# A second block of 1 to 32 slots in float32 on four column tiles, between the products of the first

## Chip, cores and metric

The kernel runs on one core of a Trainium2 chip. The metric is the device time of one execution in microseconds (us), the median of several runs. TensorE is PE in the profile (its weight loads are PEld), VectorE is DVE, ScalarE is ACT, GpSimd is POOL, and SyncE (SP) issues most of the DMAs.

## What is computed

Three stages follow one another: a linear attention over 2 x 768 tokens, a feed-forward layer with a leaky activation, and a mixture of 8 experts in which each token goes to one expert. The change touches the last stage only:

```python
logits = x @ w_gate                      # x: 1536 x 384, w_gate: 384 x 8
expert_idx = np.argmax(logits, axis=1)
...
for i in range(N):                       # capacity is 384 slots of an expert
    e = expert_idx[i]
    if counts[e] < capacity:
        disp[e, counts[e]] = x[i]
        ...
h = np.maximum(np.einsum('ecd,edf->ecf', disp, w1), 0.0)   # w1: 8 x 384 x 1024
y = np.einsum('ecf,efd->ecd', h, w2)                       # w2: 8 x 1024 x 384
out[i] = gate_w[i] * y[expert_idx[i], pos[i]]              # for the tokens kept
```

## The kernel before

Attention and the feed-forward layer run first, woven together. Each token's row, with its gate weight and its number, is scattered to `disp` in DRAM at the slot of its expert. One block of 128 slots of expert 0 is done early, beside the routing of the last tokens (class `Early`). Then a loop over the experts 0 to 7 (L1118) does the rest in blocks of 128 slots.

`expert(e, val)` runs the first block of an expert always, and a second and a third one only if the count on the chip, `val`, says so (`more`, the `tc.If` of L847, nested). Every engine reads the count into a register (`values_load`, L1125) and branches by itself. There is no loop on the chip: the code of all blocks stands in a row and is jumped over where it is not wanted.

`expert_block` works in two float32r parts (a high and a low part of each operand, three products for each pair, `PASS`). On PE a block is, in this order: `hidden(0)`, nine products of 128x128 by 512 columns (L775); five products of `hidden(1)`; `turn(0)`, four transposes (L784); the last four of `hidden(1)`; the transposes of the next expert's rows (`prep`, L658, `pd`); `second`, 24 products by 384 columns (L799) with `turn(1)` between them. ACT does the ReLU (L779) and the high part `hh` of the turned hidden values (L789), DVE their low part `hl` (L790) and at the end `y`, the output times the gate weight (L683), which POOL sends to `out` by an indirect DMA (L684).

Beside the first block of expert e the weights of expert e+1 are split into high and low parts: eight casts on ACT (L674) and eight differences on DVE and POOL (L677). The raw float32 weights (`re`) come by four DMAs of 768 KB for an expert (`load_expert`, L392 and L395), and behind them the expert's rows by one DMA (`load_rows`, L644, `drow`). All are issued in order by SP for expert e+2, ahead of expert e's own code; two experts' raw weights fit (even experts in one place, odd ones in another), so a load waits on SP until expert e's raw weights have been split. That happens during expert e-1.

The order on each engine is the order of the code (`manual_schedule`). A buffer that is used again makes its new writer wait for its last readers. In PSUM, the pool `acc` has four banks, `h` and `att` two each; in SBUF the tag `cv` has two buffers.

## Time and profile before

| what | value |
|---|---|
| median of 3 runs | 466.79 us (466.41 to 467.15) |
| the profiled execution | 466.23 us, span 464.5 us |
| PE busy | 437.4 us, 94% of the span |
| DVE, ACT, POOL busy | 271.0, 208.2, 157.7 us |
| the experts' loop (from expert 0's first product) | from 317.1 us on |

The page says how long each engine was busy and what its idle time waited for. PE is busy nearly throughout, so the time follows what PE has to do and the gaps in which it has nothing ready. Views that list instructions in order of time give a start, a length, and in brackets the idle time before them with what ended it; merged rows carry a count (x14). The length of a merged row runs to the end of its last instruction, and PE's products overlap, so the pitch of n products is the length less one product's own, over n - 1.

### The profile page before, as it was taken

Reading aid. Unit: us, or ns where it says so; the run is one execution under the profiler, and the core shown is the slowest. Engines: PE = TensorE matmul, PEld = TensorE weight load, DVE = VectorE, ACT = ScalarE, POOL = GpSimd, SP = SyncE. Lnnn points to the kernel's source line nnn. Section 1 sums busy time; section 2 is a strip of 40 time slices with the busy share of each in tenths; the row PEclk is TensorE's granted clock in tenths of the full one; section 3 lists DMA queues with packets and bytes.
Section 4 is the critical chain, followed back from the end, with each engine's and each line's share of the span. In section 5 each row is a group of like instructions: output and inputs, shape, how many; then the busy total and the mean of one; then the engine's idle time right before and its main releaser. Section 6 shows DMA issues by size and latency. Waiting matters only on the chain. (4 is left out here: it accounts for less than half of the span.)

```text
span 464.5 us, 7861 instructions
## 1 busy us (share of the span) xinstructions
PE 437.4 (94%) x3039; PEld 385.1 (83%) x3039; DVE 271.0 (58%) x470; ACT 208.2 (45%) x344; POOL 157.7 (34%) x138
## 2 busy tenths in 40 slices
PE   7977799699899999999999999999999999999995
PEld 6766699588788988989988888987988889898884
DVE  6998998999753444445333665354463535452651
ACT  1236634354344333323244444336473646553761
POOL 6855457464440231100300030033343515241660
PEclk9999979989999999999999999999999999999999
DMA  6999950649610207101700020018956556580200
GB/s 129 229 281 250 318 157 4 183 158 361 172 30 15 52 2 233 57 0 43 299 1 1 0 87 0 1 56 290 382 178 239 188 169 212 172 271 35 72 10 25
DMA packets 70605, 62.28 MB, mean 134 GB/s; under 512 B 41935, under 2 KB 58239, under 8 KB 70561
## 3 DMA queue, kind: packets, MB, share of 16 engines
q1 hardware_dynamic: 68832, 57.29, 41.1%
q0 software_dynamic: 1728, 4.40, 2.5%
q8 instruction: 28, 0.46, 0.4%
q14 instruction: 17, 0.13, 0.1%
HBM read 49.99 MB, written 12.62 MB: 135 GB/s over the span
## 5 line engine op out<-in xcount | busy, mean ns | idle before, releaser
L584 PE MATMUL acc<-wm,gh 128*128 128x384 f32 x384 | 102.0, 347 | 0.5 <-POOL wm L368 0.5
L599 PE MATMUL h<-xh,wm 128*128 128x512 f32 (+1 forms) x294 | 86.2, 402 | 4.4 <-DVE gl L622 4.4
L618 DVE SCALAR_TENSOR_TENSOR h<-ng,sign,h 128x512 f32<-128x512 f32 x48 | 36.1, 752 | 68.2 <-ACT ng L615 68.2
L584 PEld LDWEIGHTS acc<-wm,gh 128*128 128x128 f32 x384 | 69.9, 191 | 4.7 <-POOL wm L368 0.8
L775 PE MATMUL eh<-we,d 128*128 128x512 f32 x252 | 65.1, 403 | 4.5 <-PEq L847 3.2
L584 PE MATMUL acc<-wm,gl 128*128 128x384 f32 x192 | 65.4, 341 | 0.0
L599 PEld LDWEIGHTS h<-xh,wm 128*128 128x128 f32 x294 | 52.6, 190 | 14.2 <-issue 2.8
L615 ACT ACTIVATE ng<-h,slope 128x512 f32<-128x512 f32 x48 | 33.1, 689 | 60.1 <-PE h L599 60.0
L775 PEld LDWEIGHTS eh<-we,d 128*128 128x128 f32 x252 | 45.7, 188 | 15.5 <-issue 4.4
L619 ACT CAST gh<-h 128x512 fp32r<-128x512 f32 x48 | 28.1, 586 | 60.8 <-DVE h L618 60.8
L674 ACT CAST we<-re 128x768 fp32r<-128x768 f32 x64 | 50.6, 839 | 9.6 <-DMA re<-in_moe_w_dram 6.8
L677 POOL TENSOR_TENSOR we<-re,we 128x768 fp32r<-128x768 f32 x21 | 40.6, 1932 | 38.5 <-ACT we L674 32.2
L790 DVE TENSOR_TENSOR hl<-pht,hh 128x512 fp32r<-128x512 f32 x28 | 19.4, 692 | 51.6 <-ACT hh L789 49.8
L368 POOL TENSOR_TENSOR wm<-rm,wm 128x768 fp32r<-128x768 f32 x16 | 32.2, 2013 | 47.4 <-ACT wm L367 43.6
L799 PE MATMUL ey<-we,hh 128*128 128x384 f32 x224 | 48.1, 346 | 0.0
L677 DVE TENSOR_TENSOR we<-re,we 128x768 fp32r<-128x768 f32 x43 | 40.3, 965 | 11.9 <-ACT we L674 8.9
L522 POOL DMA_INDIRECT disp<-rows,sl x12 | 12.6, 1051 | 99.9 <-DVE run L543 64.4
L599 PE MATMUL h<-xl,wm 128*128 128x512 f32 (+1 forms) x147 | 42.1, 395 | 0.1
L622 DVE TENSOR_TENSOR gl<-h,gh 128x512 fp32r<-128x512 f32 x48 | 33.0, 687 | 15.6 <-ACT gh L619 15.6
L799 PEld LDWEIGHTS ey<-we,hh 128*128 128x128 f32 x224 | 37.8, 189 | 0.3 <-ACT hh L789 0.3
L584 PEld LDWEIGHTS acc<-wm,gl 128*128 128x128 f32 x192 | 36.6, 191 | 0.0
L599 PEld LDWEIGHTS h<-xl,wm 128*128 128x128 f32 x147 | 27.7, 191 | 7.0 <-DVE xl L270 0.3
(181 smaller groups left out, 618.8 us busy)
## 6 DMA issues: line engine op xcount, KB each, us to landing
re<-in_moe_w_dram SPq DMA_DIRECT2D x32, 768.0 KB, 7.2
rm<-in_moe_w_in_dram SPq DMA_DIRECT2D x8, 768.0 KB, 8.1
rm<-in_moe_w_out_dram SPq DMA_DIRECT2D x8, 768.0 KB, 7.5
disp<-rowss SPq DMA_DIRECT2D x1, 4825.0 KB, 16.0
drow<-disp SPq DMA_DIRECT2D x7, 579.0 KB, 3.9
out_dram<-rowss SPq DMA_DIRECT2D x1, 2304.0 KB, 22.4
kn<-in_k_dram SPq DMA_DIRECT2D x10, 192.0 KB, 4.6
rn<-in_r_dram SPq DMA_DIRECT2D x10, 192.0 KB, 4.8
```

Of the source, the lines that this page charges most:

```text
L368: eng.tensor_tensor(lo, low.bitcast(F32), hi.bitcast(F32), ALU.subtract)
L584: nc.tensor.matmul(accs[(blk, s)], gs[g][a][:, s * P:(s + 1) * P], wout[b][:, ft % 2, :], start=(ft == 0 and n == 0), stop=(ft == NFT - 1 ...
L599: nc.tensor.matmul(phs[g][:, cols[0]:cols[1]], win[a][:, c, o:o + P], xs[b][:, c, cols[0]:cols[1]], start=(n == 0), stop=(n == 3 * DC - 1))
L615: nc.scalar.activation(ng, ph, AF.Relu, scale=slope[:, ft:ft + 1])
L618: nc.vector.scalar_tensor_tensor(ph, ng, sign[:, ft:ft + 1], ph, op0=ALU.mult, op1=ALU.add)
L619: nc.scalar.copy(gh, ph)
L622: nc.vector.tensor_tensor(gl, ph, gh.bitcast(F32), ALU.subtract)
L674: nc.scalar.copy(t[:, sl], src[:, sl])
L677: le.tensor_tensor(t[:, sl2], src[:, sl], t[:, sl].bitcast(F32), ALU.subtract)
L775: nc.tensor.matmul(ph[q], d[x][:, c, :], ww[y][:, c, :], start=(n == 0), stop=(n == 3 * DC - 1))
L790: nc.vector.tensor_tensor(hl, pt, hh.bitcast(F32), ALU.subtract)
L799: nc.tensor.matmul(py, hT[q][x][:, c * P:(c + 1) * P], ww[y][:, c, :], start=(q == 0 and not low and c == 0 and y == 0), stop=(q == 1 and ...
```

## The change

A block of few slots gets a form of its own. Where the count of an expert is above 128 and at most 160, its second block (1 to 32 slots) is computed from the raw float32 weights, without high and low parts:

- `prep` copies the first 32 columns of the second block's turned rows to `dS` (DVE, one copy for each expert).
- `Short.hidden`: the 1024 hidden values of 32 slots are made as four column tiles of PE, each 32 columns of the array wide and each with 256 of the hidden values: 12 float32 products of 128x32 by 256 columns. `Short.relu` (ACT) and `Short.turn` (two transposes on PE, a DVE copy) prepare the second layer.
- `Short.second`: eight float32 products of 128x32 by 384 columns, again on four tiles, each tile a quarter of the sum over the hidden values. ACT copies the four quarters to `part`, and `Short.gather` adds them by one more product with `sel`, a matrix of four unit matrices that POOL makes at the start. Then a `y` of 32 rows and an indirect DMA.
- These steps stand between the steps of the first block's `front` (its `hidden` and `turn(0)`). `rest` is what is left of a block.
- `counts` now holds 0 for 129 to 160 slots and the count plus one otherwise (three small DVE operations more). Each expert branches on it in front of its first block: If (0) runs `front` with `Short`, Else runs `front` alone. So the code of the front stands there twice. The test for further blocks is `val > b * P + 1`; it fails for 0.
- `load_expert(e + 2)` and `load_rows(e + 2)` move from ahead of expert e to behind its front, since `Short` reads the raw weights that the load overwrites.

```diff
-                nc.vector.tensor_scalar(counts, pt[:, 0:E], float(cap), None, op0=ALU.min)
-                nc.vector.scalar_tensor_tensor(counts[:, 0:1], pt[:, 0:1], float(cap), sofar[:, 0:1],
+                c, few = cnt[:, 0], cnt[:, 1]
+                nc.vector.tensor_scalar(c, pt[:, 0:E], float(cap), None, op0=ALU.min)
+                nc.vector.scalar_tensor_tensor(c[:, 0:1], pt[:, 0:1], float(cap), sofar[:, 0:1],
                                                op0=ALU.min, op1=ALU.subtract)
+                nc.vector.scalar_tensor_tensor(few, c, float(P + CW), c, op0=ALU.is_le, op1=ALU.mult)
+                nc.vector.tensor_scalar(few, few, float(P), None, op0=ALU.is_le)
+                nc.vector.scalar_tensor_tensor(counts, c, 1.0, few, op0=ALU.add, op1=ALU.mult)
...
+            if b == 1:
+                dS[e] = p2.tile([P, DC, CW], F32, tag="ds", name=f"ds{e}")
+                nc.vector.tensor_copy(dS[e], src[:, :, 0:CW])
...
-    def put(rows, b, acc, name):
+    def put(rows, b, acc, name, n=P):
...
-        nc.vector.tensor_scalar(y, acc, rows[:, b, DM:DM + 1], None, op0=ALU.mult)
-        ins = nc.gpsimd.indirect_dma_start(out, bass.IndirectOffsetOnAxis(rows[:, b, DM + 1:DM + 2].bitcast(I32), 0), y, None,
-                                           bounds_check=NT - 1, oob_is_err=False)
+        nc.vector.tensor_scalar(y[0:n], acc[0:n], rows[0:n, b, DM:DM + 1], None, op0=ALU.mult)
+        ins = nc.gpsimd.indirect_dma_start(out, bass.IndirectOffsetOnAxis(rows[0:n, b, DM + 1:DM + 2].bitcast(I32), 0), y[0:n],
+                                           None, bounds_check=NT - 1, oob_is_err=False)
...
+        ph = [bank(f"eh{nm}_{q}", "h") for q in range(2)]
+        h = {0: p2.tile([P, HF], F32, tag="ng", name=f"hs{nm}_0")}
+        hT = {0: [p3.tile([P, HF], F32R, tag=t, name=f"{t}{nm}_0") for t in ("gh", "gl")]}
...
+        def front(few=None):
+            if few:
+                few.hidden()
+            hidden(0, 0, 3 * DC)
+            if few:
+                few.relu()
+            also(0)
+            relu(0)
+            if few:
+                few.turn()
+            hidden(1, 0, 5)
+            put_h0 = turn(0)
+            if few:
+                few.second()
+            also(1)
+            put_h0()
+            hidden(1, 5, 3 * DC)
+            if few:
+                few.gather()
+        def rest():
+            also(2)
+            relu(1)
+            also(3)
+            py = ps_acc.tile([P, DM], F32, tag="acc", name=f"ey{nm}")
+            second(py, 0, False, range(3))
+            put_h1 = turn(1)
+            put_h1()
+            second(py, 0, False, range(3, HF // P))
+            second(py, 0, True)
+            also(4)
+            second(py, 1, False)
+            second(py, 1, True)
+            put(dsp[e], b, py, nm)
+        return front, rest
+    class Short:
+        def __init__(self, e):
+            self.e = e
+            self.w = [raws[("e", e, q)].rearrange("p (c f) -> p c f", c=DC if q < 2 else HF // P) for q in range(NPIECE)]
...
+        def hidden(self):
+            n = F2 // NCT
+            self.ph = bank(f"eh{self.e}_s", "acc")
+            for c in range(DC):
+                for j in range(NCT):
+                    q, o = j * n // HF, j * n % HF
+                    nc.tensor.matmul(self.ph[j * CW:(j + 1) * CW, 0:n], dS[self.e][:, c, :], self.w[q][:, c, o:o + n],
+                                     start=(c == 0), stop=(c == DC - 1), skip_group_check=True)
+        def relu(self):
+            n = F2 // NCT
+            self.h = p2.tile([P, DM], F32, tag="cv", name=f"hs{self.e}_s")[:, 0:n]
+            nc.scalar.activation(self.h, self.ph[:, 0:n], AF.Relu)
+        def turn(self):
+            n = F2 // NCT
+            pt = bank(f"pht{self.e}_s")
+            for c in range(n // P):
+                nc.tensor.transpose(pt[:, c * P:(c + 1) * P], self.h[:, c * P:(c + 1) * P], ident)
+            self.hT = p2.tile([P, DM], F32, tag="cv", name=f"hT{self.e}_s")[:, 0:n]
+            nc.vector.tensor_copy(self.hT, pt[:, 0:n])
+        def second(self):
+            n = F2 // NCT // P
+            self.pp = bank(f"ey{self.e}_s", "acc")
+            for c in range(n):
+                for j in range(NCT):
+                    k = j * n + c
+                    nc.tensor.matmul(self.pp[j * CW:(j + 1) * CW, 0:DM], self.hT[:, c * P + j * CW:c * P + (j + 1) * CW],
+                                     self.w[2 + k * P // HF][:, k % (HF // P), :],
+                                     start=(c == 0), stop=(c == n - 1), skip_group_check=True)
+            self.part = p2.tile([P, DM], F32, tag="cv", name=f"part{self.e}")
+            nc.scalar.copy(self.part, self.pp[:, 0:DM])
+        def gather(self):
+            py = bank(f"es{self.e}")
+            nc.tensor.matmul(py[0:CW, 0:DM], sel, self.part, start=True, stop=True)
+            put(dsp[self.e], 1, py[:, 0:DM], f"{self.e}_s", CW)
...
-        expert_block(e, 0, beside)
+        front, rest = expert_block(e, 0, beside)
+        with tc.If(val < 1) as cmp:
+            front(Short(e))
+        with cmp.Else():
+            front()
+        if e + 2 < E:
+            for q in range(NPIECE):
+                load_expert(e + 2, q)
+            load_rows(e + 2)
+        rest()
 
         def more(b):
-            with tc.If(val > b * P):
+            with tc.If(val > b * P + 1):
                 got = []
-                expert_block(e, b, {2: [lambda: got.append(prep(e, b + 1))], 4: [lambda: got[0]()]} if b + 1 < SB else {})
+                for f in expert_block(e, b, {2: [lambda: got.append(prep(e, b + 1))], 4: [lambda: got[0]()]} if b + 1 < SB else {}):
+                    f()
...
+        nc.gpsimd.tensor_tensor(sel, ident[:, 0:CW], ident[:, CW:2 * CW], ALU.add)
+        for j in range(2, NCT):
+            nc.gpsimd.tensor_tensor(sel, sel, ident[:, j * CW:(j + 1) * CW], ALU.add)
...
         for e in range(E):
             if e + 1 < E:
                 claim(e + 1)
-            if e + 2 < E:
-                for q in range(NPIECE):
-                    load_expert(e + 2, q)
-                load_rows(e + 2)
-            val = nc.values_load(counts[0:1, e:e + 1], min_val=0, max_val=NT)
+            val = nc.values_load(counts[0:1, e:e + 1], min_val=0, max_val=1 + NT)
             expert(e, val)
```

On PE, expert 2's first block, before (eh: hidden products, pht: turned hidden values, pd: next expert's rows turned, ey: output):

```order
L1125 TENSOR_LOAD counts_105
L775 MATMUL eh2_0_0_3776<-we2_0_3470,d0_2_3468 128x512 x6
L775 MATMUL eh2_0_0_3776<-we2_0_3470,d1_2_3469 128x512 x3
L775 MATMUL eh2_0_1_3792<-we2_1_3471,d0_2_3468 128x512 x5
L784 MATMUL pht2_0_0_3798<-ident_87,hs2_0_0_3790 128x128 x4
L775 MATMUL eh2_0_1_3792<-we2_1_3471,d0_2_3468 128x512
L775 MATMUL eh2_0_1_3792<-we2_1_3471,d1_2_3469 128x512 x3
L658 MATMUL pd3_0_3813<-ident_87,drow3_3480 128x128 x3
L658 MATMUL pd3_1_3817<-ident_87,drow3_3480 128x128 x3
```

and after, the If side (eh2_s, pht2_s, ey2_s and es2 are the short block's):

```order
L1212 TENSOR_LOAD counts_105
L923 COMPARE_AND_BRANCH
L869 MATMUL eh2_s_3930<-re2_0_3326,ds2_3727 32x256 x12
L788 MATMUL eh2_0_0_3924<-we2_0_3553,d0_2_3551 128x512 x6
L788 MATMUL eh2_0_0_3924<-we2_0_3553,d1_2_3552 128x512 x3
L881 MATMUL pht2_s_3959<-ident_87,hs2_s_3952 128x128 x2
L788 MATMUL eh2_0_1_3925<-we2_1_3554,d0_2_3551 128x512 x5
L798 MATMUL pht2_0_0_3969<-ident_87,hs2_0_0_3926 128x128 x4
L892 MATMUL ey2_s_3974<-re2_2_3329,hT2_s_3962 32x384 x8
L788 MATMUL eh2_0_1_3925<-we2_1_3554,d0_2_3551 128x512
L788 MATMUL eh2_0_1_3925<-we2_1_3554,d1_2_3552 128x512 x3
L900 MATMUL es2_3993<-part2_3983,sel_107 32x384
```

The short block's products stand in four places of the first block's front, its first ones at the very start of the expert. The second block's own code is still there, behind the test of L934.

On SP, the loads for expert 7 before, issued ahead of expert 5's count and branches:

```order
L392 DMA re7_0_4594<-in_moe2_w1_dram 128x3x512 x2
L395 DMA re7_2_4597<-in_moe2_w2_dram 128x4x384 x2
L644 DMA drow7_4600<-disp_107 128x3x386
L1125 TENSOR_LOAD counts_105
L1125 ISA x2
```

and after:

```order
L1212 TENSOR_LOAD counts_105
L1212 ISA x2
L923 COMPARE_AND_BRANCH
L923 UNCONDITIONAL_BRANCH x2
L396 DMA re7_0_5091<-in_moe2_w1_dram 128x3x512 x2
L399 DMA re7_2_5094<-in_moe2_w2_dram 128x4x384 x2
L654 DMA drow7_5097<-disp_109 128x3x386
L934 COMPARE_AND_BRANCH x2
```

The four weight loads and the rows' load behind them have moved past the branch of expert 5's front; they now also wait for PE to have left that front.

On ACT, the start of expert 2 before (we3: the next expert's weights, hs: ReLU, hh: high part):

```order
L1125 TENSOR_LOAD counts_105
L674 CAST we3_0_3750<-re3_0_3474 128x768 x2
L779 ACTIVATE hs2_0_0_3790<-eh2_0_0_3776 128x512
L674 CAST we3_1_3751<-re3_0_3474 128x768
L789 CAST hh2_0_0_3803<-pht2_0_0_3798 128x512
```

and after, the If side:

```order
L1212 TENSOR_LOAD counts_105
L923 COMPARE_AND_BRANCH
L875 ACTIVATE hs2_s_3952<-eh2_s_3930 128x256
L687 CAST we3_0_3906<-re3_0_3679 128x768 x2
L793 ACTIVATE hs2_0_0_3926<-eh2_0_0_3924 128x512
L896 COPY part2_3983<-ey2_s_3974 128x384
L687 CAST we3_1_3907<-re3_0_3679 128x768
L804 CAST gh2_0_0_3927<-pht2_0_0_3969 128x512
```

The short block's ReLU now stands ahead of the first casts, and its copy of the quarters ahead of the cast and of the first block's high part.

## Rows read from the trace of the kernel before

**Rows 1.** The page: busy time of PE, and its granted clock in 40 slices
```profile
PE 437.4 (94%) x3039; PEld 385.1 (83%) x3039; DVE 271.0 (58%) x470; ACT 208.2 (45%) x344; POOL 157.7 (34%) x138
PEclk9999979989999999999999999999999999999999
```

**Rows 2.** Busy time by stretch (experts 1, 6); columns: length, then each engine, clock, DMA
```profile
337.70:358.20 20.50, 19.70 (x109) 17.50 (x109) 9.83 (x14) 11.78 (x20) 7.75 (x5) 1.00 0.66 219
438.80:449.60 10.80, 10.18 (x56) 8.91 (x56) 7.84 (x11) 9.08 (x14) 7.39 (x5) 1.00 0.04 13
```

**Rows 3.** PE in order of time (start, length, idle before): expert 1, expert 2's start
```profile
337.68 3.50 PE L775 MATMUL eh<-we,d 128*128 128x512 f32 x14 [0.79 <-PEq L847]
...
341.38 1.17 PE L775 MATMUL eh<-we,d 128*128 128x512 f32 x4
...
347.66 1.56 PE L775 MATMUL eh<-we,d 128*128 128x512 f32 x6
...
358.24 2.11 PE L775 MATMUL eh<-we,d 128*128 128x512 f32 x8 [0.84 <-PEq L847]
```

**Rows 4.** PE in order of time: expert 6, of one block, and expert 7's start
```profile
438.83 3.54 PE L775 MATMUL eh<-we,d 128*128 128x512 f32 x14 [0.59 <-ACTq L847]
...
443.59 0.82 PE L658 MATMUL pd<-ident,drow 128*128 128x128 f32 x6
...
449.61 2.61 PE L775 MATMUL eh<-we,d 128*128 128x512 f32 x10 [0.59 <-ACTq L847]
```

**Rows 5.** The page's groups: hidden products, ACT's casts (count, busy us, mean ns, idle)
```profile
L775 PE MATMUL eh<-we,d 128*128 128x512 f32 x252 | 65.1, 403 | 4.5 <-PEq L847 3.2
...
L674 ACT CAST we<-re 128x768 fp32r<-128x768 f32 x64 | 50.6, 839 | 9.6 <-DMA re<-in_moe_w_dram 6.8
```

**Rows 6.** PE in order of time: float32 products of the attention, whole array and parts
```profile
18.09 1.13 PE L218 MATMUL py<-S,rT 128*128 128x96 f32 x8 [0.49 <-ACT kT L202]
...
20.81 1.16 PE L209 MATMUL pa<-scratch,kT 64*128 64x128 f32 x16
...
25.95 0.64 PE L236 MATMUL pg<-scratch,kd 128*64 128x48 f32 x16
26.51 1.16 PE L209 MATMUL pa<-rT,scratch 64*128 64x128 f32 x16
...
30.38 1.14 PE L225 MATMUL py<-scratch,scratch 128*64 128x48 f32 x32
```

**Rows 7.** The source lines of two of them: shortest, median and longest in ns
```profile
L209 PE MATMUL pa<-scratch,kT x16: 272/272/373, 20.8 to 21.7; 64*128 64x128 f32 x16
L225 PE MATMUL py<-scratch,scratch x32: 222/222/257, 30.4 to 31.3; 128*64 128x48 f32 x32
```

**Rows 8.** The source view of L847: the compare and branch on PE's sequencer, in ns
```profile
L847 PEldq COMPARE_BRANCH  x18: 70/181/339, 325.6 to 457.5; - x18
```

**Rows 9.** DVE and POOL in order of time at expert 6's start: the end of expert 5
```profile
439.08 0.61 DVE L683 TENSOR_SCALAR y<-ey,drow 128x384 f32<-128x384 f32 x1
...
441.04 1.52 POOL L684 DMA_INDIRECT out_dram<-y,drow  x1 [0.16 <-issue]
```

**Rows 10.** DVE's groups by shape: a small copy
```profile
L448 DVE COPY lg<-pl 128x8 f32<-128x8 f32 x8 | 1.3, 159 | 2.2 <-PE pl L446 2.2
```

**Rows 11.** The source view of L684: landing times of the output DMAs
```profile
DMA to landing us min/median/max: 2.1/3.2/7.4
```

**Rows 12.** The source view of L392, 405 to 415 us: two loads for expert 7
```profile
DMA to landing us min/median/max: 4.6/5.3/6.1
```

**Rows 13.** The source view of L392, 315 to 316 us: two loads behind others
```profile
L392 SPq DMA_DIRECT2D re<-in_moe_w_dram x2: 487/488/488, 315.3 to 315.9; - x2
...
DMA to landing us min/median/max: 8.3/9.1/9.8
```

**Rows 14.** The page's DMA issues: KB of each, us to landing
```profile
re<-in_moe_w_dram SPq DMA_DIRECT2D x32, 768.0 KB, 7.2
...
drow<-disp SPq DMA_DIRECT2D x7, 579.0 KB, 3.9
```

More of the change, by code (lines that the diff above doesn't have):

```diff
@@ L100 @@
     counts = const.tile([P, E], I32, name="counts")
+    cnt = const.tile([P, 2, E], F32, name="cnt")
+    sel = const.tile([P, CW], F32, name="sel")
     sofar = const.tile([P, 2], F32, name="sofar")
@@ L784, in turn @@
                 nc.tensor.transpose(pt[:, c * P:(c + 1) * P], h[q][:, c * P:(c + 1) * P], ident)
-            hh = p3.tile([P, HF], F32R, tag="gh", name=f"hh{nm}_{q}")
-            hl = p3.tile([P, HF], F32R, tag="gl", name=f"hl{nm}_{q}")
+            if q not in hT:
+                hT[q] = [p3.tile([P, HF], F32R, tag=t, name=f"{t}{nm}_{q}") for t in ("gh", "gl")]
+            hh, hl = hT[q]
             def f():
```

33 lines of the change are left out of this document (6 added, 27 removed).

## The prediction, made before the run

> **What bounds the kernel now.** I read the page first: PE is busy 94% of the span and its granted clock is full in all late slices [rows 1], so time is what PE executes plus its gaps. Then the stretches of the experts: in expert 1, of two blocks, PE is busy 19.70 of 20.50 us and no other engine over 11.78; in expert 6, of one block, PE 10.18 of 10.80 and ACT 9.08 [rows 2]. The reader should see that PE is the bound in both, but that ACT has little room in an expert of one block. PE's list of instructions gives the steps: expert 1 runs from 337.68 to 358.24, 20.56 us, its second block begins at 347.66 without a gap, and the next expert begins 0.84 after PE fell idle, put down to the branch [rows 3]. Expert 6 runs from 438.83 to 449.61, 10.78 us with its gap of 0.59 [rows 4].
>
> Which experts change is in the data: the reference's own inputs route, after expert 0's early block and the cut at 384, 256, 132, 159, 141, 384, 57, 118 and 53 tokens to experts 0 to 7. So experts 1, 2 and 3 have second blocks of 4, 31 and 13 slots, all of them within 32; expert 4 keeps three blocks and expert 0 two.
>
> **What is removed.** A second block with its share of the gap is 20.56 - 10.78 = 9.78 us on PE. Three make 29.3.
>
> **What PE gets instead.** Price of one column first. In float32r, 14 products of 512 columns take 3.50 [rows 3], one alone 0.403 [rows 5]: a pitch of (3.50 - 0.40)/13 = 0.238, or 0.465 ns a column. A float32 product leaves two records. On two row tiles, 16 records of 128 columns take 1.16 us and one alone 0.272 [rows 6, 7]: eight pairs, (1.16 - 0.27)/7 = 0.127 for a pair, at most 0.99 ns a column if two run at once. On the whole array eight records of even fewer columns (96) take 1.13 [rows 6], a pitch of (1.13 - 0.27)/7 = 0.122 for one record against 0.064 for one on tiles. So tiles do run at once, nearly two for one. No row shows four tiles or a float32 product long enough to separate its columns from its weight load; a column is between 0.465 and 0.99 ns for each record. I take 0.93, twice the float32r price, as the nearest float32 row is close to it.
>
> With four at once: hidden, 3 rounds x 2 records x 256 x 0.93 = 1.43. Second layer, 2 x 2 x 384 x 0.93 = 1.43. Gather, 2 x 384 x 0.93 = 0.71. Two transposes at (0.82 - 0.27)/5 = 0.11 [rows 4], 0.22. Going from one division of the array to another: the last record of L236 starts near 25.95 + 0.64 - 0.22 = 26.37 and L209 begins at 26.51 [rows 6, 7], 0.14 instead of a pitch of 0.03, so 0.11 each; six of them, 0.66. Together 4.45 for an expert, 13.35 for three. At 0.465 a column it would be 2.66.
>
> The trace shows 1.9 of 2 for two tiles. The Trainium skill (TensorE: Matmul & The Clock Gate, Measured speedup vs the span model) gives 2.38 for three column tiles of 32, 0.79 of the ideal; by that the 2.86 of hidden and second layer would be 3.6 and the total 2.3 later, an estimate that no run here shows.
>
> **The new branch.** All eight experts now branch on PE ahead of their first product, right behind the count's load, when PE has run dry. One takes 0.18, at most 0.34 [rows 8]; the target lies behind some 30 to 90 instructions. I take 0.25, together 2.0. The ends are nothing (PE's sequencer is ahead of the array where 347.66 follows without a gap) [rows 3] and twice 0.34 for two branches, 5.4. The jump at the front's end has four products queued ahead of it and costs nothing; without that cover it is within the same bound.
>
> **Waits that the short block brings.** (1) Its hidden products stand first and take a bank of the pool `acc`, eight allocations to an expert on four banks, so it is the bank of the previous expert's output, free only after `y`. That ends at 439.08 + 0.61 = 439.69, 0.86 after expert 6's start [rows 9, 4]. Ahead of it DVE now has the copy of `dS`: 96 elements, between a copy of 8 (0.16) [rows 10] and `y` of 384 (0.61), by interpolation 0.27. PE is ready 0.25 after the old start, so it waits about 0.9, with all of the expert queued behind. This holds in experts 2 and 3, whose predecessor ends with that block: 1.8. Expert 1's predecessor had a second block since, so nothing. Ends: 0 and 3.
> (2) `hT` takes a `cv` buffer from which the previous `y` is still being sent: POOL starts that DMA 2.2 after the expert's start [rows 9, 4] and it lands 3.2 later, from 2.1 to 7.4 [rows 11]: at 5.4, from 4.3 to 9.6. DVE wants the buffer some 5.8 after the start (0.9, the short hidden, nine products, two transposes, two differences on DVE). I take nothing; the other end is 3.8 in each of two experts, with the first block's `hl` behind it on DVE.
> (3) ACT's copy of the quarters (at most 0.61) waits for the second layer, and a cast of 0.84 [rows 5] and `hh` stand behind it; PE has four products, the gather and six transposes for that time. I take nothing, at most 0.6 in each of three.
> DVE's three operations on the counts lie beside the early block's products, POOL's three for `sel` beside the attention's first loads; at the start of PE's work each would cost no more than a `y`.
>
> **The loads that moved.** Before, the loads for expert 7 were issued at 406.7 [rows 12], within expert 4. Now SP waits until PE has left expert 5's front, 341.38 + 1.17 - 337.68 = 4.87 after its start [rows 3]. The first piece lands after 4.6 [rows 12]. Loads in a queue land one behind the other: two issued 0.5 apart land after 8.3 and 9.8, so 2.0 apart [rows 13]. The fourth lands after 10.6, and the rows, 579 against 768 KB [rows 14], 1.5 later, 12.1. That is 17.0 after expert 5's start. Expert 6 wants the rows for its `pd` at 443.59 - 438.83 = 4.76 after its own start [rows 4], which is 10.78 + 0.25 later: 15.8. PE waits 1.2 there, with the first block's second layer behind it. The weights are earlier than ACT's casts want them. Ends: 0, and 5 if the first piece takes 8.3 [rows 13]. In experts 1 to 3 the loads start about 8 after an expert's start and have 15.5 of its length: the rows land near 20, wanted at 20.5 or later, so no wait. Expert 4 has three blocks of cover.
>
> **The sum.** -29.3 + 13.35 + 2.0 + 1.8 + 1.2 = -10.95. The profiled execution took 466.23 us with a span of 464.5; the median is 0.56 above it, and I take the difference from the median: 466.79 - 10.95 = 455.8.
>
> **Rivals.** Cheaper columns: at 0.465 ns three experts save 3 x 1.79 = 5.4 more, 450.4. For it: the float32 rows bound a column only from above. Against it: L209's pair stands close to 0.99.
> Two tiles at once, not four: hidden and second layer double, 3 x 2.86 = 8.6, 464.4. For it: no row has more than two.
> One tile after another, the case on the other side: 12 and 8 products instead of 3 and 2 rounds, 5.71 each, 3 x 8.56 = 25.7 more, 481.5. It decides from 10.95/3 = 3.65 us more for an expert, that is 6.5 for what would be 11.4 in a row: fewer than 1.75 tiles at once. Against it stand 0.064 and 0.122 [rows 6].
> Late data: the bounds of the output DMA or of the loads come true in part, 4 to 7 more, near 461.
> A jump that must fetch code: were each of the eight branches to wait for a DMA, at the shortest landing of 2.1 [rows 11], 8 x 2.1 = 16.8 instead of 2.0, 470.6. Against it: the jump over an unexecuted block in expert 6's end is inside a gap of 0.59 [rows 4]. The Trainium skill (Runtime: NRT & Kernel Launch, Instruction fetch mechanics) states that a taken branch to a page not loaded waits for a fetch.
> The short form is not taken, if the chip counts otherwise: 466.79 + 2.0 + 1.2 = 470.
>
> **How the numbers follow.** Forecast 0.60, cheaper columns 0.13, two at once 0.09, late data 0.08, one after another 0.05, fetch 0.03, not taken 0.02. A measurement here tells about 0.2% from no change. The first four are faster by more, 0.90, less 0.01 for the mishaps of two at once and late data together that end near 466: faster 0.89, same 0.02, slower 0.09. The range 449.5 to 464.0 holds the forecast (alone 453 to 459), cheaper columns, late data and the better half of two at once.
>
> **What would show it.** Right: 11 full blocks in the hidden products' count (198 instead of 252 for L775's successors), experts 1 to 3 lasting 15.5, 16.4 and 16.4, four records of a short product starting within hundredths of a microsecond, a wait of PE for `y` at the start of experts 2 and 3, and one for `drow` of about 1.2 in expert 6. Wrong: short products whose records follow one another, gaps over 1 us at the branch, or a wait for `re`.

## The result, and the profile after

The changed kernel takes 462.03 us (median of five runs, 461.06 to 463.93) where the kernel before took 467.08 on the same chip: a ratio of 0.9897, 95% interval 0.9872 to 0.9923. It is faster by 5.0 us; the sum of the prediction said 10.95. The profiled execution took 462.03 us, with a span of 459.9.

The page of the changed kernel first: busy time of the engines, PE's granted clock in 40 slices, and the group of the full blocks' hidden products (count, busy us, mean ns, idle before).

```profile
PE 424.0 (92%) x3012; PEld 363.5 (79%) x3012; DVE 267.9 (58%) x475; ACT 201.7 (44%) x335; POOL 160.0 (35%) x141
...
PEclk9998999989999999999999999999999899899999
...
L788 PE MATMUL eh<-we,d 128*128 128x512 f32 x198 | 54.5, 420 | 5.4 <-ACT we L687 3.1
```

Beside [rows 1, 5]: 198 hidden products stand where 252 stood, so three second blocks did take the short form. PE is busy 13.4 us less, but its share of the span went down from 94 to 92%, so waits came; the mean of one hidden product went from 403 to 420 ns, and two late slices of the clock are below 9, which before had none.

PE in order of time, experts 1 to 4 (start, length, idle before and what ended it), beside [rows 3]. L869 is the short block's hidden layer, L892 its second layer, L788 the full block:

```profile
337.67 1.50 PE L869 MATMUL eh_s<-re,ds 128*32 128x256 f32 x24 [0.99 <-DVEq L934]
...
343.22 1.50 PE L892 MATMUL ey_s<-re,hT_s 128*32 128x384 f32 x16
...
353.92 1.62 PE L869 MATMUL eh_s<-re,ds 128*32 128x256 f32 x24 [1.89 <-DVEq L934]
...
361.84 2.10 PE L892 MATMUL ey_s<-re,hT_s 128*32 128x384 f32 x16 [2.15 <-DVE hT_s L883]
...
373.84 1.50 PE L869 MATMUL eh_s<-re,ds 128*32 128x256 f32 x24 [1.66 <-DVEq L934]
...
380.24 1.50 PE L892 MATMUL ey_s<-re,hT_s 128*32 128x384 f32 x16 [0.78 <-DVE hT_s L883]
...
392.12 5.04 PE L788 MATMUL eh<-we,d 128*128 128x512 f32 x14 [3.08 <-ACT we L687]
```

Expert 1 lasts 16.25 us from start to start (15.5 forecast), expert 2 19.92 and expert 3 18.28 (16.4 forecast for each); expert 4 takes 30.37, 1.6 more than before. The short block itself is as forecast: 24 records in 1.50 us. What is new stands in the brackets. In experts 2 and 3 the second layer waits for the turned hidden values, and these, on DVE, for the DMA of `y`, which POOL had issued 6.2 us earlier in expert 2 (from 355.17 to 361.36) and 4.7 us earlier in expert 3; ACT's copy is held behind that. The last two rows are SP's, the loads of expert 4's weights:

```profile
355.17 1.00 POOL L697 DMA_INDIRECT out_dram<-y,drow  x1 [0.16 <-issue]
...
361.36 0.42 DVE L883 COPY hT_s<-pht_s 128x256 f32<-128x256 f32 x1 [2.61 <-DMA out_dram<-y,drow]
379.76 0.42 DVE L883 COPY hT_s<-pht_s 128x256 f32<-128x256 f32 x1 [1.10 <-DMA out_dram<-y,drow]
...
364.04 0.48 ACT L896 COPY part<-ey_s 128x384 f32<-128x384 f32 x1 [5.50 <-PE ey_s L892]
...
352.15 1.10 SPq L396 DMA_DIRECT2D re<-in_moe_w_dram  x2
353.30 1.23 SPq L399 DMA_DIRECT2D re<-in_moe_w_dram  x2
```

Stretches of PE (length, busy time of PE, PEld, DVE, ACT and POOL, then PE's granted clock, DMA share, GB/s): the wait in expert 2, what came behind it, expert 4's first products, and a stretch of expert 4 later on.

```profile
358.00:361.80 3.80, 1.68 (x10) 1.16 (x8) 1.17 (x2) 0.54 (x1) 0.00 (x0) 1.00 1.05 399
362.60:366.00 3.40, 3.40 (x17) 1.33 (x10) 0.23 (x1) 1.70 (x3) 0.66 (x1) 0.50 0.59 179
...
393.30:396.70 3.40, 3.40 (x9) 2.68 (x9) 0.41 (x1) 1.31 (x2) 0.41 (x1) 0.50 0.90 313
404.00:414.00 10.00, 10.00 (x57) 8.95 (x56) 3.83 (x7) 3.05 (x6) 2.84 (x2) 1.00 0.06 22
```

The clock is at its lower level, 1.2 GHz, in two stretches, each behind a wait of PE: the 2.15 us in expert 2 and the 3.08 at expert 4's start. There 14 products take 5.04 us instead of 3.50 [rows 3]. The first row also shows the DMA engines full (a share of 1.05) while the output DMA is on its way: expert 4's weights had been issued in the 3 us ahead of it.

The 3.08 us at expert 4 are put down to ACT, but ACT had only its usual casts. The source view of the branch (PE's queue, ns) and the instruction queue's DMA between 389.4 and 390.6 us (packets, MB, share) show what PE did then:

```profile
L923 PEldq COMPARE_BRANCH  x1: 2307/2307/2307, 389.6 to 389.6; - x1
```
```profile
q8 instruction: 1, 0.02, 5.6%
```

PE's own branch took 2.31 us, with one packet of code moving in the first half of it; its other ten L923 branches took 0.07 to 0.33.

### The profile page after: what moved, and what is told of

It is laid out like the page before. It is cut to its first block, busy times and chain, and to the rows that moved or that the text cites. A ratio compares the mean times of both kernels' runs of the same rounds, so it can differ in the third digit from the quotient of the medians.

```text
span 459.9 us, 7878 instructions
## 1 busy us (share of the span) xinstructions
PE 424.0 (92%) x3012; PEld 363.5 (79%) x3012; DVE 267.9 (58%) x475; ACT 201.7 (44%) x335; POOL 160.0 (35%) x141
## 5 line engine op out<-in xcount | busy, mean ns | idle before, releaser
L593 PE MATMUL acc<-wm,gh 128*128 128x384 f32 x384 | 100.8, 343 | 0.5 <-POOL wm L372 0.5
L608 PE MATMUL h<-xh,wm 128*128 128x512 f32 (+1 forms) x294 | 87.4, 407 | 3.6 <-DVE gl L631 3.6
L593 PEld LDWEIGHTS acc<-wm,gh 128*128 128x128 f32 x384 | 68.8, 188 | 4.9 <-POOL wm L372 1.1
L788 PE MATMUL eh<-we,d 128*128 128x512 f32 x198 | 54.5, 420 | 5.4 <-ACT we L687 3.1
L690 POOL TENSOR_TENSOR we<-re,we 128x768 fp32r<-128x768 f32 x21 | 41.7, 1984 | 50.8 <-ACT we L687 36.0
L788 PEld LDWEIGHTS eh<-we,d 128*128 128x128 f32 x198 | 37.2, 197 | 17.3 <-issue 9.9
L805 DVE TENSOR_TENSOR gl<-pht,gh 128x512 fp32r<-128x512 f32 x22 | 15.2, 692 | 44.1 <-ACT gh L804 42.4
L813 PE MATMUL ey<-we,gh 128*128 128x384 f32 x176 | 37.7, 346 | 0.0
L813 PEld LDWEIGHTS ey<-we,gh 128*128 128x128 f32 x176 | 29.7, 189 | 0.4 <-ACT gh L804 0.4
```

Source lines behind the costliest of these rows:

```text
L593: nc.tensor.matmul(accs[(blk, s)], gs[g][a][:, s * P:(s + 1) * P], wout[b][:, ft % 2, :], start=(ft == 0 and n == 0), stop=(ft == NFT - 1 ...
L608: nc.tensor.matmul(phs[g][:, cols[0]:cols[1]], win[a][:, c, o:o + P], xs[b][:, c, cols[0]:cols[1]], start=(n == 0), stop=(n == 3 * DC - 1))
L690: le.tensor_tensor(t[:, sl2], src[:, sl], t[:, sl].bitcast(F32), ALU.subtract)
L788: nc.tensor.matmul(ph[q], d[x][:, c, :], ww[y][:, c, :], start=(n == 0), stop=(n == 3 * DC - 1))
L805: nc.vector.tensor_tensor(hl, pt, hh.bitcast(F32), ALU.subtract)
L813: nc.tensor.matmul(py, hT[q][x][:, c * P:(c + 1) * P], ww[y][:, c, :], start=(q == 0 and not low and c == 0 and y == 0), stop=(q == 1 and ...
```

## Experiments

Three theories were to be told apart: the missing gain went into waits for buffers (and the clock behind them); into the branch; or the short block's products or loads cost more than the sum had. The times of all runs, each with the kernel before measured beside it (its times differ by up to 1.6 us, so the ratios compare best):

| run | us | before | ratio, 95% interval |
|---|---|---|---|
| changed kernel | 462.03 | 467.08 | 0.9897 (0.9872 to 0.9923) |
| own_buf | 456.77 | 466.76 | 0.9789 (0.9773 to 0.9805) |
| own_both | 460.12 | 466.76 | 0.9869 (0.9852 to 0.9887) |
| not_taken | 469.69 | 466.76 | 1.0071 (1.0054 to 1.0088) |
| fixed | 457.99 | 466.76 | 0.9827 (0.9799 to 0.9856) |
| ds_act | 462.42 | 466.90 | 0.9911 (0.9882 to 0.9941) |
| ds_act_bank | 465.36 | 466.90 | 0.9970 (0.9951 to 0.9988) |
| swap | 455.21 | 466.90 | 0.9751 (0.9709 to 0.9793) |
| fixed_buf | 451.92 | 466.90 | 0.9676 (0.9656 to 0.9695) |
| pool_tail | 456.27 | 466.35 | 0.9796 (0.9772 to 0.9819) |
| swap_pool | 454.20 | 466.35 | 0.9741 (0.9720 to 0.9763) |
| shift | 457.64 | 465.63 | 0.9832 (0.9805 to 0.9859) |
| serial, e3_long, late_loads | 462.71, 461.38, 457.85 | 466.35, 467.26, 467.26 | one run each |

**own_buf: the short block's values out of y's buffers.**

```diff
-            self.hT = p2.tile([P, DM], F32, tag="cv", name=f"hT{self.e}_s")[:, 0:n]
+            self.hT = p2.tile([P, HF], F32, tag="ng", name=f"hT{self.e}_s")[:, 0:n]
...
-            self.part = p2.tile([P, DM], F32, tag="cv", name=f"part{self.e}")
+            self.part = p2.tile([P, HF], F32, tag="ng", name=f"part{self.e}")[:, 0:DM]
```

> Edit: the short block's turned hidden (hT_s) and its part sum (part) lie in buffers of the ng group, which holds no row that goes out by DMA, instead of in the two cv buffers that they share with y. Nothing else changes, and nothing is left out. Theory (the missing gain went into waits for y's DMA and what followed from them): the waits of ey_s for hT_s, 2.15 us in expert 2 and 0.78 in expert 3, go to 0; the ACT copy to part is no longer held (5.50 and 3.52 us before it become about 2.5, as in expert 1); and the half-speed stretch of the granted clock at 362.6 us, which came after the 2.15 us wait, goes with it (second products 1.50 instead of 2.10 us, the next four hidden products 1.2 instead of 2.08). 462.0 - 2.9 - 1.5 = 457.6 us. Rival (the clock falls for another reason, by what the experts' loop as a whole does): the clock still falls once in experts 1 to 3, 459.1 us. Rival (the DMA wait only covers another one, such as late weights): ey_s waits for another name, 461 to 462 us. The 3.08 us ahead of expert 4 stay in all three.

Measured: 456.77 us, 5.3 less than the changed kernel (4.9 when each is set against its own before). PE, DVE and ACT of own_buf in order of time:

```profile
354.24 1.50 PE L869 MATMUL eh_s<-re,ds 128*32 128x256 f32 x24 [1.91 <-DVEq L934]
...
359.80 1.50 PE L892 MATMUL ey_s<-re,hT_s 128*32 128x384 f32 x16
...
387.81 4.99 PE L788 MATMUL eh<-we,d 128*128 128x512 f32 x14 [3.23 <-ACT we L687]
```
```profile
358.69 0.42 DVE L883 COPY hT_s<-pht_s 128x256 f32<-128x256 f32 x1
```
```profile
361.41 0.48 ACT L896 COPY part<-ey_s 128x384 f32<-128x384 f32 x1 [2.66 <-PE ey_s L892]
```

No bracket is left ahead of L892, DVE copies at once, ACT is held for 2.66 instead of 5.50, and the 2.10 us of L892 are 1.50 again: the clock stays up there. The wait for y's DMA and the clock behind it were the largest part of what was missing: 5.3 us by the medians, 4.4 by the rows (waits of 2.15 and 0.78, and 1.5 of lower clock: from the start of L892 to that of L900 it is 4.03 us in expert 2 and 2.55 in expert 1). Why this DMA was late, the trace of before tells. Its 15 output DMAs fall into two groups: six, issued 0.1 to 0.5 us behind a weight load, landed after 5.9 to 7.4 us; nine, issued over 7 us behind one, after 2.1 to 3.5. The source view of L684 of before, at 350.6 us and at 358.3:

```profile
DMA to landing us min/median/max: 6.5/6.5/6.5
```
```profile
DMA to landing us min/median/max: 2.1/2.1/2.1
```

**own_both: another PSUM bank for the short hidden layer as well.**

```diff
-            self.ph = bank(f"eh{self.e}_s", "acc")
+            self.ph = bank(f"eh{self.e}_s")
```

> Edit: as the kernel with the buffers of its own, and eh_s lies in one of the two att banks instead of an acc bank. Nothing is left out. Theory (what PE waits for at the start of experts 2 and 3 over the branch is y's read of the acc bank): the gaps ahead of eh_s, 0.99, 1.89 and 1.66 us, all come to about 1.0, so 0.9 + 0.7 = 1.6 us less than with the buffers alone: 457.6 - 1.6 = 456.0 us, which is about what the prediction gave, plus the 3 us wait at expert 4. Rival (the branch itself is longer there, on PE or on DVE's side of it): the gaps stay at 1.9 and 1.7, and the time is that with the buffers alone.

The gaps ahead of `eh_s` are 1.09, 2.02 and 1.74 us: nothing gained, so the bank that the prediction named is not what holds PE there. The time is even 3.4 us above own_buf's. The trace has the reason, a second long branch of PE (2.95 us, the jump over the unused blocks at expert 5's end), and the clock down behind it. PE at expert 6's start:

```profile
429.96 5.05 PE L788 MATMUL eh<-we,d 128*128 128x512 f32 x14 [2.23 <-PEq L934]
```

**not_taken: the same program, short form never chosen.** The threshold is a constant in the kernel.

```diff
-                nc.vector.scalar_tensor_tensor(few, c, float(P + CW), c, op0=ALU.is_le, op1=ALU.mult)
+                nc.vector.scalar_tensor_tensor(few, c, 0.0, c, op0=ALU.is_le, op1=ALU.mult)
```

> Edit: the count's test is set so that no expert counts as few (0 in the place of 160), so the same program takes the Else side in all eight experts, and the second blocks of experts 1 to 3 run as full blocks again. The output is complete. It prices the branch with its two sides and the loads behind it, without the short blocks. Against before: eight branches at the 0.25 us of the prediction are 2.0 us, so 467.1 + 2.0 = 469.1 us. If the 2.31 us that PE's branch took at expert 4 is a fetch of code behind the weight loads that go at the same time, it is seen again at one or more of the eight: each adds about 2.1 us, 469 to 476 us, and PE's branch rows show values of about 2 us at those experts. If it belongs to what came before it in the changed kernel (the short block, the jump over its Else side), all branch rows are 0.07 to 0.35 us, and the time is 468 to 469.5.

The branch, its two sides and the moved loads cost 2.9 us over before, 0.37 for each expert. No branch is long, in the source view of L923 (shortest, median, longest ns); then PE at expert 4's start, in not_taken and in before:

```profile
L923 PEldq COMPARE_BRANCH  x8: 214/288/435, 316.5 to 452.3; - x8
```
```profile
401.48 3.52 PE L788 MATMUL eh<-we,d 128*128 128x512 f32 x14 [1.44 <-ACT we L687]
```
```profile
399.32 3.50 PE L775 MATMUL eh<-we,d 128*128 128x512 f32 x14 [0.80 <-PEq L847]
```

So the long one does not come with jumping to the long side as such.

**fixed and fixed_buf: the choice written into the program**, in the changed kernel and in own_buf.

```diff
-        with tc.If(val < 1) as cmp:
-            front(Short(e))
-        with cmp.Else():
-            front()
+        if e in (1, 2, 3):
+            front(Short(e))
+        else:
+            front()
```

> Edit: the choice between the two sides is written into the program (experts 1, 2 and 3 short, the others without), with no branch on the chip for it; buffers and banks stay as in the changed kernel. The output is complete for these counts. It prices the branch in the program with the short blocks. Theory: the 3.08 us ahead of expert 4 are PE's branch, which took 2.31 us there, so the wait goes down to about 0.8 us, the clock does not fall behind it (1.6 us), and the other seven starts are 0.2 to 0.4 us shorter: 462.0 - 2.3 - 1.6 - 2.0 = 456.1 us; with the clock falling all the same, 457.7. Rival (PE waits there for ACT's casts of the weights, as the trace's releaser says): the 3 us stay, and the time is 462.0 - 2.0 = 460.0 us. The waits for hT_s in experts 2 and 3 stay as they are.

> Edit: as own_buf, with the choice written into the program (experts 1, 2 and 3 short) and no branch for it on the chip. Complete for these counts. It is the changed kernel without its waits for y's DMA and without its branch, so what is left against before is the short block's own work: three blocks less at 9.78 us, three short ones at 4.2 to 4.45, and the waits for DVE ahead of eh_s (0.9 and 0.9): 466.8 - 29.3 + 13.0 + 1.8 = 452.3 us. Against own_buf: expert 4's wait 3.23 to 0.56 and its clock 1.5, the starts of experts 1, 2, 6 and 7 0.2 to 0.7 shorter each: 456.8 - 5.9 = 450.9 us. Rival (waits that the branch covers come up once it is gone): 454 us or more, with a new name ahead of PE.

fixed took 457.99 us. Expert 4's wait went to 0.56 us, and the clock did not fall there, so the wait was PE's branch and not ACT's casts; but the clock fell in expert 2, where the wait for `hT_s` grew to 2.49 us, and to 1.97 in expert 3: there the output DMAs landed 6.3 and 5.7 us after their issue. fixed_buf has neither those waits nor the branch and took 451.92 (452.3 by the sum of the prediction's terms, 450.9 from own_buf). PE at the starts of experts 3 and 4:

```profile
370.29 1.50 PE L869 MATMUL eh_s<-re,ds 128*32 128x256 f32 x24 [1.71 <-DVEq L934]
...
385.20 3.55 PE L788 MATMUL eh<-we,d 128*128 128x512 f32 x14 [0.56 <-ACTq L934]
```

The branch costs 4.85 us in own_buf, and without it 1.7 us ahead of `eh_s` are still there.

**ds_act and ds_act_bank: who makes the short block's float32 columns**, in own_buf and with the bank of own_both.

```diff
-                nc.vector.tensor_copy(dS[e], src[:, :, 0:CW])
+                nc.scalar.copy(dS[e], src[:, :, 0:CW])
```

> Edit: as own_buf, and the copy of the short block's 32 float32 columns (ds) is made by ACT instead of DVE; eh_s stays in an acc bank. Nothing is left out. In own_buf PE waited 1.91 and 1.63 us ahead of eh_s in experts 2 and 3, for DVE. Theory A (it waits for DVE because ds is DVE's, and that wait is met only once DVE has done the y behind it): with ds on ACT the gaps fall to about 1.1 us, 456.8 - 0.8 - 0.5 = 455.5 us. Theory B (the acc bank that y reads, as predicted, and ds besides): the gaps stay near 1.9 and 1.6 here and fall only where the bank is moved too; here 456.8 us. The 3.2 us ahead of expert 4 stay in both.

> Edit: as ds_act, and eh_s lies in an att bank instead of an acc bank. Nothing is left out. own_both, with the bank alone, left the gaps ahead of eh_s at 2.02 and 1.74 us. Theory A (ds alone): the same gaps as ds_act, about 1.1 us, and the same time, 455.5 us. Theory B (bank and ds together): gaps of 1.1 us here and not in ds_act. If the 2.95 us branch that own_both had ahead of expert 6 came from the bank, it is here again, and the time is 3.5 to 4 us longer; if it came from chance in when code is fetched, it can be gone.

Both expectations fell: the gaps rose to 2.65 and 2.71 us in ds_act, 2.85 and 2.91 in ds_act_bank. ACT and DVE of ds_act at expert 1's end show why, and what PE waits for:

```profile
351.45 0.24 ACT L677 COPY ds<-pd 128x96 f32<-128x96 f32 x1 [0.92 <-DVE d L674]
351.59 2.30 ACT L687 CAST we<-re 128x768 fp32r<-128x768 f32 x3
352.46 1.83 DVE L690 TENSOR_TENSOR we<-re,we 128x768 fp32r<-128x768 f32 x2 [1.04 <-ACT we L687]
...
354.20 0.61 DVE L696 TENSOR_SCALAR y<-ey,drow 128x384 f32<-128x384 f32 x1
354.88 0.82 PEld L869 LDWEIGHTS eh_s<-re,ds 128*32 128x32 f32 x18 [2.94 <-ACTq L934]
```

ACT's copy waited for DVE, its casts came later, DVE's two differences behind them too, and `y` behind those ended at 354.81; PE began at once after. In own_buf `y` ended at 354.19 and PE began at 354.24. In these runs PE starts when DVE's queue of the expert before is empty, whichever engine makes `ds`. Other starts became later too (1.81 us ahead of experts 6 and 7), and the clock fell behind four waits of the profiled ds_act, which is where its 5.7 us over own_buf lie. ds_act_bank has a long branch at expert 5's end again (3.00 us), so that one came with the bank both times. Which operand carries the wait is not settled: each variant left PE something that DVE reads or writes.

**pool_tail: less for DVE at the end of an expert** (own_buf).

```diff
-                      4: [lambda: [g() for g in got], *split((2, 1, V), (3, 0, V), (3, 1, G))]}
+                      4: [lambda: [g() for g in got], *split((2, 1, V), (3, 0, G), (3, 1, G))]}
```

> Edit: as own_buf, and of the last three splits of the next expert's weights one (the first half of the fourth piece) has its low part made by POOL instead of DVE. Nothing is left out. ds_act showed that PE's wait ahead of eh_s has nothing to do with who copies ds: with ds on ACT it rose to 2.65 us, as DVE's splits came later. Theory (at the start of experts 2 and 3 PE waits until DVE is through with its queue of the expert before, whose last two splits and y end 1.9 us after PE's last product): with one split less, 0.95 us, y comes right after PE's last product, and the gaps fall from 1.91 and 1.63 to 1.1 to 1.2 us: 456.8 - 1.3 = 455.5 us. Rival (POOL, with four splits an expert, becomes late itself: its puts and the weights for the second products): new waits for POOL or DMA, 457 us or more. Expert 4's 3.2 us stay.

The gaps fell to 1.04 and 0.83 us, more than expected. DVE and PE of pool_tail at expert 2's start:

```profile
353.83 0.60 DVE L696 TENSOR_SCALAR y<-ey,drow 128x384 f32<-128x384 f32 x1
...
354.49 1.94 PE L869 MATMUL eh_s<-re,ds 128*32 128x256 f32 x24 [1.04 <-DVEq L934]
```

So DVE's queue was the cause of these gaps. The time gained less than the gaps: 456.27 us, runs from 455.11 to 457.37, which doesn't stand clear of own_buf; its 24 records at expert 2 took 1.94 instead of 1.50 us, and the long branch is still there.

**swap: the long side first in the program** (own_buf).

```diff
-        with tc.If(val < 1) as cmp:
-            front(Short(e))
-        with cmp.Else():
-            front()
+        with tc.If(val > 0) as cmp:
+            front()
+        with cmp.Else():
+            front(Short(e))
```

> Edit: as own_buf, with the two sides of the branch in the other order in the program: the side without the short block first, the side with it second. The same work is done. Theory (at expert 4 PE jumps over the short side into code that was not yet there, 2.39 us of branch): expert 4 now runs into its side without a jump at its start, its branch row falls to under 0.4 us and its wait from 3.23 to about 1.2, the granted clock does not fall there (4.99 us for 14 products become 3.5): 456.8 - 2.0 - 1.5 = 453.3 us if nothing new comes. Now experts 1 to 3 jump at their starts: each that meets the same costs 2 us, and 3.5 with the clock, so one of them gives 456 to 457 us and three 460 to 464. Rival (expert 4's wait has to do with the loads of expert 6 that start at the same time, whichever way PE goes): the 3.2 us stay at expert 4.

455.21 us (runs from 453.06 to 456.63), where 453.3 was forecast if nothing new came. The source view of L923 at expert 4 and at expert 2, then PE at expert 4:

```profile
L923 PEldq COMPARE_BRANCH  x1: 70/70/70, 386.5 to 386.5; - x1
```
```profile
L923 PEldq COMPARE_BRANCH  x1: 1403/1403/1403, 353.9 to 353.9; - x1
```
```profile
386.69 3.51 PE L788 MATMUL eh<-we,d 128*128 128x512 f32 x14 [0.84 <-ACTq L934]
```

Expert 4's wait and the clock's fall are gone; a branch of 1.40 us came at expert 2, mostly beside the wait for DVE (2.16 instead of 1.91 us). That jump is not the first to the second side of the branch: expert 1's was, at 0.23 us, and expert 3's took 0.22. Another long row, 1.41 us, is the jump over the unused blocks at expert 5's end.

**shift, e3_long, late_loads: what makes that branch long.** All on own_buf: 64 products in a side that is never run, ahead of expert 1's code; expert 3 sent to the long side; expert 6's weights loaded later, from ACT's queue.

```diff
+            for _ in range(64 if self.e == 0 else 0):
+                nc.tensor.matmul(self.ph[:, 0:P], ident, ident, start=True, stop=True)
...
+                nc.vector.memset(few[:, 3:4], 1.0)
...
-                load_expert(e + 2, q)
+                load_expert(e + 2, q, nc.scalar if e == 4 else None)
```

> Edit: as own_buf, with 64 more products of the identity put into expert 0's short side. Expert 0 has 256 rows and never takes that side, so nothing more is done; only PE's code behind it lies further back. Theory (the 2.39 us branch of PE at expert 4 is a jump into code that has not been fetched, and which jump it is goes by where the code lies in the packets of 16 KB that PE's instruction queue fetches): the long branch row at expert 4 goes or moves to another jump, and the 3.23 us wait with it. With none left on the path: 456.8 - 2.0 - 1.5 = 453.3 us; with one at another place, 455 to 457; with one more, 458 to 460. Rival (expert 4's jump is slow whatever its place, as it is the first to the long side after short experts, or as it meets the loads of expert 6): the 2.3 to 2.4 us stay at expert 4, 456.8 us.

> Edit: as own_buf, with the chip's choice for expert 3 set to the long side, so that its 13 rows run as a full second block again; experts 1 and 2 stay short. Complete output. Case A (the first jump to the long side after a short expert is the slow one, as the code that was fetched ahead was the short expert's way): the 2.3 us branch moves from expert 4 to expert 3, and expert 4's is under 0.45 us. Case B (it is expert 4's place in the code or its loads): it stays at expert 4 with 2 us or more. Time in both: a full block at 9.78 us for a short one at 4.2, 456.8 + 5.6 = 462.4 us.

> Edit: as own_buf, with the loads of expert 6's weights issued from ACT's queue behind ACT's work of expert 4's first part, instead of from SP's queue, where they go out 0.5 us ahead of PE's branch at expert 4. Nothing is left out. Case L (the fetch of code is slow because it stands behind those loads): the branch falls from 2.39 to about 1.1 to 1.3 us, what one packet of code takes by itself, the wait from 3.23 to about 2.1, and with no fall of the clock the time is 456.8 - 1.1 - 1.5 = 454.2 us. Case N (the loads have no part in it): 2.2 to 2.4 us again, 456.8 us, or more if the later loads hold up expert 6.

The branch rows of shift, then of late_loads, then of e3_long at expert 3 and at expert 4:

```profile
L925 PEldq COMPARE_BRANCH  x11: 72/178/2233, 316.7 to 440.3; - x11
```
```profile
L924 PEldq COMPARE_BRANCH  x11: 73/178/2345, 315.5 to 440.7; - x11
```
```profile
L924 PEldq COMPARE_BRANCH  x1: 1366/1366/1366, 369.2 to 369.2; - x1
```
```profile
L924 PEldq COMPARE_BRANCH  x1: 336/336/336, 392.9 to 392.9; - x1
```

The loads have no part in it: they went out 7.5 us later, and the branch took 2.35 us. shift leaves it at expert 4 too, but it is no test of the place. A float32 product is two records, each with its weight load, so 64 products are 256 instructions; the instruction queue moved one packet of 16 KB more than in own_buf, and those behind it started at the same points of the program (385.3 against 385.1 us ahead of expert 4). So the code seems to have moved by a whole packet, with its places within the packets unchanged. The two pages:

```profile
q8 instruction: 32, 0.52, 0.4%
```
```profile
q8 instruction: 33, 0.54, 0.5%
```

With expert 3 on the long side, the long branch moves to expert 3 and expert 4's is short; the time, 461.38 us, is near the 462.4 of both cases. So in this order of the sides it is the first jump to the long side behind experts that ran the short one. swap shows that this is no rule for other programs. The Trainium skill (Runtime: NRT & Kernel Launch, Instruction fetch mechanics) says that an engine fetches its code ahead in sequence and that a taken branch out of what it holds waits for a fetch. The traces agree: in all runs here PE has 16 branches of over 1 us, and each ends 2.4 to 2.7 us after a packet of code started to move (the changed kernel's at 389.47, its branch over at 391.96; swap's at 352.75 and 355.33; e3_long's at 367.84 and 370.52). That is also why one row shows 2.3 us and another 1.4: in the first the jump came with its packet, in the second some 1.2 us after it. Which jumps meet this, and whether the place of the code decides it, stays open.

**serial: one column tile's products after another's** (own_buf; the loops over tiles and chunks change places).

```diff
-            for c in range(DC):
-                for j in range(NCT):
+            for j in range(NCT):
+                for c in range(DC):
```

> Edit: as own_buf, with the short block's products in another order: all chunks of one column tile, then all of the next, instead of the four tiles in turn. The same products are made. Theory (the four tiles work at the same time only when products on different tiles follow each other): hidden's 24 products take four times 1.43 us instead of 1.50, ey_s's 16 four times 1.43, so each short block is 8.6 us longer, and with three of them the time is 456.8 + 25.7 = 482.5 us, as in the prediction's case of products one after another. Rival (the order in the program does not matter, what counts is that four tiles have work queued): 456.8 us.

Neither expectation held: 462.71 us. PE in expert 1 of serial:

```profile
338.15 2.86 PE L869 MATMUL eh_s<-re,ds 128*32 128x256 f32 x24 [0.98 <-DVEq L934]
...
345.06 1.52 PE L892 MATMUL ey_s<-re,hT_s 128*32 128x384 f32 x16
```

The hidden layer takes 2.86 us, not 5.7, and the second layer 1.52, as with tiles in turn: 24 records at 0.216 us each, the pitch of one tile, would take over 5 us, so PE starts a later tile's products while the earlier tile's are still running. The order is worth 1.4 us a block, 4.1 in all; of the rest of the 5.9 us over own_buf, 1.0 is in that one run's clock at expert 4 (6.01 us for 14 products, own_buf 4.99).

**swap_pool: the two edits that helped, together.**

> Edit: as swap (the side without the short block first), with that split on POOL as well. Nothing is left out. swap was 455.2 us with waits of 1.21, 2.16 and 1.63 us ahead of the three eh_s and a branch of 1.40 us ahead of expert 2. Theory (DVE's late queue): the waits at experts 2 and 3 fall to 1.1 to 1.2, where PE's branch ends early enough, 455.2 - 1.3 = 453.9 us. Rival (the 1.40 us branch holds PE at expert 2 by itself): 2.0 stays there, 1.2 at expert 3, 454.8 us. POOL late: 455.5 us or more.

454.20 us, 12.2 below before, where the changed kernel is 5.0 below its own: the fastest version here that still chooses on the chip. Expert 3's gap is 0.97 us; at expert 2 the branch, 1.60 us now, holds PE for 2.37, as the rival had it.

## Why the prediction came out too large

Right in direction, and in the range, but the gain was 5.05 us where the sum said 10.95. Step by step:

- **Removed, -29.3, and the short block, +13.35: right.** Expert 1's block is 14.36 us, from 337.67 to 353.92 less its 1.89 of idle, against 10.19 for a single block [rows 4]: 4.2 us for a short block, forecast 4.45. fixed_buf, 15.0 below its before, confirms both together with 1.8 us of waits ahead of `eh_s` (14.15 by the sum). Four tiles do run at once, and each layer took 1.50 us where the price of 0.93 ns a column gave 1.43; the two together took 3.00, not the 3.6 of the prediction's other estimate.
- **The branch, +2.0: too small.** not_taken measured 2.9 in all; and at expert 4, behind three short experts, the branch is long, which makes the wait there 3.08 us instead of not_taken's 1.44, 1.6 more, with 1.5 us of lower clock behind it. The rival "a jump that must fetch code" was priced for all eight branches; it came true for one.
- **Term (1), a wait for y's bank, +1.8: the size right, the reason only in part, so the size was partly luck.** Over expert 1's 0.99 the gaps were 0.90 and 0.67 us longer, and they end with `y`, as forecast. But another bank left them, and fewer differences on DVE took them away: PE waits until DVE is through with the expert before. A short expert has the same splits in 14 us that a full one has in 20, and they end after PE.
- **Term (2), `hT` and y's output DMA, taken as nothing: the step that failed.** Its own bound of 3.8 in each of two experts was open. The forecast was a DMA through 5.4 us after the expert's start and a DVE that wants the buffer at 5.8. In expert 2 the DMA was through after 7.4 and DVE was ready after 4.8. I took the median landing of 3.2 us [rows 11], which is that of the DMAs with no load near them. The prediction had the loads start about 8 us after an expert's start, clear of this DMA. Expert 4's did not wait for the short block; SP issued them from 352.15 on, when PE was done with expert 1, and the DMA issued behind them at 355.17 took 6.2 us. The waits were 2.15 and 0.78 us, and the first brought the clock down, 1.5 more that no term had. own_buf gives 5.3 us back for the whole.
- **Term (3), ACT's copy of the quarters, 0: right.** Held for 2.7 us in own_buf, it delays nothing on PE.
- **The moved loads, +1.2 for `drow` in expert 6: did not come.** I let SP wait for PE's front in expert 5. But SP issued expert 7's first load at 422.96, 0.47 us into expert 5, not 4.87, and the rows at 429.50, and PE's transposes in expert 6 follow without a gap at 438.35. The likely reason is that only the short side reads the raw weights; no run tests it.

In sum, against the profiled executions' difference of 4.2 us (4.6 between their spans): -29.3 + 12.5 for three short blocks + 2.9 branch + 1.6 ahead of `eh_s` + 2.9 for `hT_s` + 1.6 for the long branch + 3.0 of lower clock comes to -4.8, near enough for terms that overlap by some tenths. The terms that the sum lacked, 7.5 us, all hang on two events: an output DMA beside loads, and one jump.

## What to carry to other kernels

A buffer that goes out by DMA is free only when that DMA has landed, here after 2.1 to 3.5 us with no load near it and after 4.7 to 7.4 with weight loads beside it; when work is moved between an output and its buffer's next use, price the landing with the loads as they will be, or give the new work a buffer that no DMA reads. A branch on the chip cost 0.37 us for each expert here, and at one jump 1.6 us more and 1.5 of lower clock: try both orders of the two sides, and look at the longest branch row, not the median. Where a step gets shorter, see whose fixed work for the next step (here DVE's weight splits) no longer fits into it.

## What the runs showed of the hardware

- Branch rows of PE are 0.07 to 0.45 us, but 1.37 to 2.45 at one jump into an expert's side in each program whose experts run different sides on the chip's choice, and in four of them 1.4 to 3.0 at a jump over unused blocks. Each of these 16 long rows ends 2.4 to 2.7 us after the start of a packet of code. Moving a PSUM bank, with the same work, was enough for one more of these (own_both, ds_act_bank).
- After a wait of PE the granted clock fell to its lower level in many cases: in the experts' loops of these traces, such a stretch began in or behind 15 of 20 waits of over 2.1 us, at some 1.5 us each where it lay behind the wait; the other five had none, pool_tail's 2.78 and ds_act_bank's 3.18 among them.
- Four column tiles worked at once on float32 products, 1.50 us for a layer with the tiles in turn. One tile after another, the layer with four records on each tile took the same (1.52), the one with six on each 2.86.
- Output DMAs of the kernel before landed after 2.1 to 3.5 us, and after 5.9 to 7.4 where a weight load had been issued up to 0.5 us ahead of them.
